# Four output stores moved behind the K loads of batch 2, with a fourth output buffer

## The chip, the cores and the metric

The kernel runs on one core of a Trainium2 chip. A core has TensorE (matrix products), VectorE, ScalarE and GpSimd, SyncE, which here only issues transfers, and 16 DMA engines that move data between HBM (the chip's memory) and SBUF (the core's). ScalarE can issue transfers too, from a queue of its own. The metric is the device time of one execution in microseconds (us); where several runs are given, their median.

In the profile PE is TensorE's product unit, PEld its loading of weights, DVE is VectorE, ACT is ScalarE, POOL is GpSimd, and SPq and ACTq are the DMA-issuing sides of SyncE and ScalarE.

## The reference

Sliding-window causal attention over eight batches of eight heads, 576 positions and 64 columns, and then a layer with a hard-swish over all 4608 positions:

```python
scores = (q @ k.transpose(0, 1, 3, 2)) / sqrt(64)        # (8, 8, 576, 576)
rel = pos[:, None] - pos[None, :]
scores = where((rel >= 0) & (rel < 64), scores, -1e9)
attn = softmax(scores)                                    # over the last axis
x = (attn @ v).transpose(0, 2, 1, 3).reshape(4608, 512)
h = x @ moe_w_in                                          # (4608, 2048)
g = h * clip(h + 3, 0, 6) / 6
out = g @ moe_w_out                                       # (4608, 512), float32
```

## The kernel before

The batches b = 0 to 7 go through attention one after the other, and the layer works on nine blocks T = 0 to 8 of 512 positions. While TensorE multiplies block T in `s1` (x by the first weight, line 767) and `s2` (by the second, line 815), the attention of batch T + 1 is slotted between the products of `s2`.

Inputs arrive as float32 in staging tiles (`st`, six of them, and `tl` for the last 64 rows of a batch), are cast to bf16, and are used from there. Batches 0 and 1 (b < NR6 = 2) are transposed on TensorE. From batch 2 on another way is taken (`load_nat`): four loads and a tail for Q, four loads and a tail for K (line 455, SyncE's queue), a cast of each on GpSimd into `nat` (line 277), and then one DMA transposition for Q and one for K from `nat` into `QKT` (line 434, SyncE's queue). The first scores of the batch (`scores64`, line 648) need both transpositions. The V of such a batch is loaded in five pieces by ScalarE's queue (`stream_v`, line 381), in gaps between its activations. The normalised output of attention (`opg`) goes through four further DMA transpositions into `xT` (line 720, SyncE), which `s1` of the next block reads.

An output tile of 128 x 512 is made in PSUM (`acc`), copied by ScalarE to an SBUF tile `osb` (line 832), and stored to HBM from SyncE's queue (line 837). `osb` has three buffers; copy number `nst` is planned behind store `nst - 3`. Each block T has four such stores; those of T = 0 are the numbers 0 to 3, called stores 1 to 4 below.

The order of the instructions on each engine is fixed when the program is built. The class `Plan` holds a list of work items, each with an engine, a time at which it is ready, a duration and the keys of the items it depends on; it simulates the engines with fixed costs and emits each item when its turn comes. `moved` is its model of the DMA queue, `pl.mark` states that a key is done, and `deps` names the keys to be waited for. An order once emitted is followed on the chip whatever the real times are: each engine takes its instructions in sequence, and an instruction that waits for a semaphore holds up all behind it. The transfers of both queues share eight completion semaphores in rotation, and a transfer waits, before it is issued, until the previous user of its semaphore has landed.

Near the change SyncE's queue before has this order: four Q loads of batch 2, store 1, Q's tail, two K loads, store 2, two K loads, store 3, K's tail, the transposition of Q, store 4, the transposition of K, and then the loads of batch 3.

Of the kernel before, what the change touches and what calls it, by code (L numbers as in the profile page):

```python
# [10 lines left out]
F32 = mybir.dt.float32  # L11
# [9 lines left out]
NSTAGE = 6  # L21
NQT = 1
NPT = 4
VGAP = 1.8
VGAP2 = 1.8
VRATE = 150
# [78 lines left out]
def kernel(  # L105
# [10 lines left out]
    P = nc.NUM_PARTITIONS  # L116
# [5 lines left out]
    KB = (S + P - 1) // P  # L122
    SP = KB * P
# [7 lines left out]
    QW = P + WINDOW  # L131
    VW = D + 1
    scale = 1.0 / math.sqrt(D)
    NR6 = 2
# [3 lines left out]
    pl = Plan()  # L138

    consts = ctx.enter_context(tc.tile_pool(name="consts", bufs=1))  # L140
# [2 lines left out]
    small = ctx.enter_context(tc.tile_pool(name="small", bufs=3))  # L143
    opool = ctx.enter_context(tc.tile_pool(name="opool", bufs=4))
    t1pool = ctx.enter_context(tc.tile_pool(name="t1", bufs=3))
    osbp = ctx.enter_context(tc.tile_pool(name="osb", bufs=3))
    psums = [ctx.enter_context(tc.tile_pool(name=f"ps{i}", bufs=1, space=PSUM)) for i in range(3)]
    early = ExitStack()
    psums.append(early.enter_context(tc.tile_pool(name="ps3", bufs=1, space=PSUM)))
# [24 lines left out]
    neg32 = consts.tile([P, QW], F32, name="neg32")  # L174
    neg = consts.tile([P, TB], BF16, name="neg")
    half = consts.tile([P, 1], F32, name="half")
    mask32 = consts.tile([P, QW], F32, name="mask32")
    m64 = consts.tile([P, D], F32, name="m64")
    mask = consts.tile([P, QW], BF16, name="mask")
    win16 = consts.tile([P, NG, FF], BF16, name="win16")  # L180
# [11 lines left out]

    P_ring = [consts.tile([P, 2, KB, 2 * P], BF16, name=f"pT{i}") for i in range(NPT)]
    V_ring = [consts.tile([P, NG, KB, 2, VW], BF16, name=f"V{i}") for i in range(2)]
# [66 lines left out]
    def stage_slot(casts):  # L261

        stage_hist.append(casts)
        return tuple(stage_hist[-1 - NSTAGE]) if len(stage_hist) > NSTAGE else ()

    def moved(now, kb, rate):

        dma["t"] = max(dma["t"], now) + kb / rate
        land = dma["t"] + 1.9 + dma["lag"]
        return max(now + 0.06, dma["t"] - 5.0), land  # L270

    def cast_op(eng, out_ap, in_ap):
        if eng == "DVE":
            return lambda s: nc.vector.tensor_copy(out=out_ap, in_=in_ap) and None  # L274
        if eng == "ACT":
            return lambda s: nc.scalar.copy(out=out_ap, in_=in_ap) and None  # L276
        return lambda s: nc.gpsimd.tensor_copy(out=out_ap, in_=in_ap) and None  # L277
# [36 lines left out]
    def tail_slot(casts):  # L314
        tail_hist.append(casts)
        return tuple(tail_hist[-4]) if len(tail_hist) > 3 else ()
# [48 lines left out]
    def stream_v(b):  # L365

        V, W = V_ring[b % 2], W_ring[b % 2]
        tiles = {}
        deps = stage_slot([("cast", b, 2, i) for i in range(KB - 1)]) + (("pv", b - 2, NG - 1), ("issued", b, 1 if b == NR6 else 0))
        tdeps = tail_slot([("cast", b, 2, KB - 1)])  # L370

        def issue(kb):
            ss = min(P, S - kb * P)
            def fn(s):
                if kb == 0:
                    tiles["t"] = stage.tile([P, 4, H * D], F32, name="st", tag="st")
                    tiles["l"] = tails.tile([P, H * D], F32, name="tl", tag="tl")
                if kb == KB - 1:
                    pl.mark(("vgo", b), s)
                st = tiles["l"][:ss, :] if kb == KB - 1 else tiles["t"][:, kb, :]  # L380
                nc.scalar.dma_start(
                    out=st.rearrange("p (h d) -> p h d", h=H),
                    in_=v[b, :, kb * P : kb * P + ss, :].rearrange("h s d -> s h d"),
                )
                dma["v"] = max(dma["v"], s) + 262 * ss / P / VRATE
                land = dma["v"] + 2.7
                sv = st.rearrange("p (g h d) -> p g h d", g=NG, h=2)
                todo = [(("POOL",), W[D:P, :, kb, :, 0:D], sv[0:D], H * D)]
                if ss == P:
                    todo.append((("POOL",), V[:, :, kb, :, 0:D], sv, H * D))  # L390
                    todo.append((("POOL",), W[0:D, :, kb + 1, :, 0:D], sv[D:P], H * D))
                casts(("cast", b, 2, kb), land, todo)
                if kb < KB - 1:
                    pl.op("ACT", s + (VGAP2 if b == NR6 else VGAP), 0.45, issue(kb + 1))
            return fn
        pl.op("ACT", 0.0, 0.45, issue(0), deps=deps + tdeps)
# [26 lines left out]
    def load_nat(b):  # L423
        for i, src in enumerate((q, k)):
            T = {"left": KB}
            n = natural[i]
            deps = stage_slot([("cast", b, i, j) for j in range(KB - 1)])
            if b > NR6:
                deps += (("vgo", b - 1),)
            if b > NR6:  # L430
                deps += (("tr", b - 1, i),)
            def tr(t, i=i, n=n):
                def fn(s):
                    nc.sync.dma_start_transpose(
                        out=QK_tiles[b % NQT][:, i * NG : (i + 1) * NG, :].rearrange("d g (k t) -> d (g k) t", t=P),
                        in_=n[:].rearrange("p g k d -> p (g k d)"),
                    )
                    fr, land = moved(s, 655, 230)
                    pl.free["SP"] = fr
                    pl.mark(("issued", b, i), s)  # L440
                    return land
                d = (("S", b - NQT, NG - 1),) if b >= NQT else ()
                if b > 2:
                    d += (("s1", b - 1),)
                pl.op("SP", t, 0.1, fn, ("tr", b, i), deps=d)
            for kb in range(KB):
                ss = min(P, S - kb * P)
                def go(s, i=i, src=src, kb=kb, ss=ss, T=T, n=n, tr=tr):
                    if kb == 0:
                        T["t"] = stage.tile([P, 4, H * D], F32, name="st", tag="st")  # L450
                    if kb == KB - 1:
                        st = tails.tile([P, H * D], F32, name="tl", tag="tl")[:ss, :]
                    else:
                        st = T["t"][:, kb, :]
                    nc.sync.dma_start(
                        out=st.rearrange("p (h d) -> p h d", h=H),
                        in_=src[b, :, kb * P : kb * P + ss, :].rearrange("h s d -> s h d"),
                    )
                    fr, land = moved(s, 262 * ss / P, 205)
                    def done(t):  # L460
                        T["left"] -= 1
                        if not T["left"]:
                            tr(t)
                    pl.op("POOL", land, 0.61,
                          cast_op("POOL", n[:ss, :, kb, :], st.rearrange("p (g d) -> p g d", g=NG)),
                          ("cast", b, i, kb), done)
                    return fr
                yield b, deps + tail_slot([("cast", b, i, kb)]) if kb == KB - 1 else deps, go
        stream_v(b)
# [59 lines left out]
    def ready(f, b, g):  # L529
# [4 lines left out]
        elif f[0] == "S":  # L534
            ks = [("tr", b, g)] if b < NR6 else [("tr", b, i) for i in range(2)]
            if b == 0:
                ks.append("neg")
            if n >= NPT:
                ks.append(("pv", (n - NPT) // NG, (n - NPT) % NG))
        elif f == "PV":  # L540
# [32 lines left out]
    def scores(b, g, which=(0, 1)):  # L573
# [3 lines left out]
        n = b * NG + g  # L577
        pT = P_ring[n % NPT]
        add = b == 0
# [53 lines left out]
    def blocks(b, g):  # L633
        n = b * NG + g
        return P_ring[n % NPT][:].rearrange("p h k w -> p (h k w)")[:, 0 : 2 * S].rearrange("p (h c) -> p h c", h=2)

# [42 lines left out]
    def pv128(b, g, o):  # L679
        V = V_ring[b % 2]  # L680
        pT = P_ring[(b * NG + g) % NPT]
        for h in range(2):
# [142 lines left out]
    def finish(T, ts, acc, c0, c1):  # L825
        u0 = T * TB + ts * P
        nst = T * 4 + ts + (c0 > 0)
        cell = {}
        def cp(s):
            osb = osbp.tile([P, DM], F32, name="osb", tag="osb")  # L830
            cell["o"] = osb
            nc.scalar.copy(out=osb[:, c0:c1], in_=acc[:, c0:c1])  # L832
            if c0:
                nc.scalar.dma_start(out=out[u0 : u0 + P, c0:c1], in_=osb[:, c0:c1])
        def store(t):
            def fn(s):
                nc.sync.dma_start(out=out[u0 : u0 + P, c0:c1], in_=cell["o"][:, c0:c1])
                fr, land = moved(s, 262, 375)
                pl.free["SP"] = fr
                return land  # L840
            pl.op("SP", t, 0.1, fn, ("st", nst))
        pl.op("ACT", pl.t + 0.1, 0.62, cp, ("acc", nst), None if c0 else store,
              deps=(("st", nst - 3),) if nst >= 3 else ())


    next_load(0.0)
# [34 lines left out]
    for T in range(NTB):  # L881
# [3 lines left out]
        b = T + 1  # L885
# [36 lines left out]
```

The softmax here doesn't subtract the row's maximum and nothing guards it: scores larger than these inputs give would overflow.

## Time and profile before

| | us |
|---|---|
| median of 5 runs | 310.81 (310.34 to 312.92) |
| the profiled execution | 311.0 |
| its span in the profile | 309.3 |
| TensorE busy | 296.4 |
| VectorE, ScalarE, GpSimd busy | 161.0, 157.0, 116.1 |

The span is the time from the first to the last instruction in the profile; 1.7 us of the profiled execution lie around it. TensorE's granted clock is 1.00 throughout. A line of the timeline gives the start, the time taken, the engine, the line of the kernel, the operation, what is written and read, the number of instructions merged, and in brackets the idle time before it with what ended it. The stretch that the change concerns, in the same profile, cut in pieces with the busy time of each engine, the clock, the share of the DMA engines and their rate:

```profile
core 0: us, PE busy (x) PEld busy (x) DVE busy (x) ACT busy (x) POOL busy (x), PEclk, DMA share, GB/s
59.20:74.00 14.80, 14.75 (x68) 6.50 (x67) 8.95 (x8) 9.20 (x9) 6.75 (x12) 1.00 1.27 248
74.00:75.20 1.20, 0.07 (x6) 0.07 (x7) 0.88 (x1) 0.29 (x1) 1.07 (x3) 1.00 1.32 201
75.20:92.00 16.80, 16.27 (x209) 8.36 (x214) 7.37 (x13) 6.43 (x11) 9.97 (x15) 1.00 1.15 201
```

TensorE is busy all the time until 74.0, does almost nothing for 1.2 us, and is nearly full again.

The transfers of SyncE around it, with the time from issue to landing where the prediction uses it:

| transfer | issued at | takes to issue | landed at |
|---|---|---|---|
| first Q load of batch 2 | 46.95 | 0.57 | 51.95 |
| store 1 | 52.12 | 1.71 | 56.5 |
| store 2 | 55.89 | 0.88 | 60.1 |
| store 3 | 58.52 | 1.36 | 63.1 |
| K's tail | 59.92 | 0.61 | 64.6 |
| transposition of Q | 60.63 | 4.19 | 68.4 |
| store 4 | 64.95 | 0.50 | 69.95 |
| transposition of K | 65.57 | 4.37 | 75.07 |
| first Q load of batch 3 | 70.46 | 0.40 | 76.96 |

### The profile page before, as it was taken

How to read it: one execution, taken by the hardware profiler on the slowest of the kernel's cores; microseconds unless marked ns; L12 is line 12 of the kernel's file. 1: busy time of each engine (PE TensorE's matmuls, PEld its weight loads, DVE VectorE, ACT ScalarE, POOL GpSimd, SP SyncE). 2: the span in 40 equal slices, each digit the busy share in tenths (PEclk: the TensorE clock that was granted, in tenths of full speed). 3: DMA queues.
4: the chain of work that ended last, by engine and by line, in shares of the span. 5: the costliest groups of instructions: out<-in, count | busy, mean ns of one | idle time of the engine just before them, and what ended most of it. 6: DMA issues, size and time to landing. Idle time of an engine off the chain costs nothing.

```text
span 309.3 us, 6664 instructions
## 1 busy us (share of the span) xinstructions
PE 296.4 (96%) x2746; PEld 153.7 (50%) x2787; DVE 161.0 (52%) x208; ACT 157.0 (51%) x199; POOL 116.1 (38%) x185
## 2 busy tenths in 40 slices
PE   8979999998999999999999999999999999999996
PEld 4544445643544454875444544444665544444443
DVE  5486675566614772468336642675176516404610
ACT  5936677465515651566155724662367236315611
POOL 3167558437824741357127622662261000000000
PEclk9999999999999999999999999999999999999999
DMA  8999999999999998999899999999990520010011
GB/s 231 279 336 389 389 311 210 256 223 238 197 220 241 253 215 161 205 233 214 178 171 257 213 183 205 250 216 159 209 208 29 120 76 0 34 70 35 0 68 70
DMA packets 153487, 58.38 MB, mean 189 GB/s; under 512 B 142064, under 2 KB 143344, under 8 KB 153456
## 3 DMA queue, kind: packets, MB, share of 16 engines
q1 hardware_dynamic: 125184, 50.80, 76.9%
q10 hardware_dynamic: 28272, 7.15, 12.0%
q8 instruction: 22, 0.36, 0.5%
q14 instruction: 9, 0.07, 0.1%
HBM read 36.70 MB, written 9.44 MB: 149 GB/s over the span
## 4 chain that ended last, share of the span: by engine, by line
PE 71%; DMA 18%; POOL 4%; SPq 3%; issue 2%; DVE 0%; ACT 0%; ACTq 0%; POOLq 0%
PE acc L815 35%; PE ps L767 29%; DMA QKT<-nat 6%; DMA st<-in_moe_w_out_dram 5%; PE ps L672 3%; DMA st<-in_v_dram 3%; PE ps L648 3%; DMA st<-in_k_dram 3%; SPq L329 1%; POOL V L277 1%; SPq L412 1%; POOL wout L277 1%; DMA out_dram<-osb 1%; PE ps L737 0%; PE ps L685 0%
## 5 line engine op out<-in xcount | busy, mean ns | idle before, releaser
L779 DVE SCALAR_TENSOR_TENSOR gT<-t,ps 128x1024 bf16<-128x1024 bf16 x72 | 87.6, 1221 | 102.0 <-ACT t L776 102.0
L815 PE MATMUL acc<-wout,gT 128*128 128x512 bf16 (+2 forms) x559 | 129.3, 373 | 3.1 <-issue 2.2
L767 PE MATMUL ps<-xT,win 128*128 128x512 bf16 (+4 forms) x696 | 126.1, 340 | 1.1 <-DVE gT L779 0.6
L776 ACT ACTIVATE t<-ps,half 128x1024 bf16<-128x1024 f32 x72 | 79.8, 1113 | 50.0 <-PE ps L767 47.8
L767 PEld LDWEIGHTS <-win 128*128 128x128 bf16 x704 | 65.2, 98 | 60.6 <-issue 1.5
L815 PEld LDWEIGHTS <-gT 128*128 128x128 bf16 x592 | 53.6, 98 | 57.9
L832 ACT COPY osb<-acc 128x512 f32<-128x512 f32 (+2 forms) x37 | 21.3, 575 | 75.9 <-PE acc L815 66.5
L277 POOL CAST runs<-st 64x512 bf16<-64x512 f32 (+1 forms) x49 | 30.8, 628 | 66.1 <-DMA st<-in_v_dram 55.9
L277 POOL CAST nat<-st 128x512 bf16<-128x512 f32 x48 | 32.1, 676 | 23.0 <-DMA st<-in_k_dram 15.4
L654 ACT ACTIVATE pT<-ps 128x640 bf16<-128x640 f32 (+1 forms) x48 | 28.7, 650 | 10.7 <-PE ps L648 10.7
L713 DVE TENSOR_TENSOR opg<-ps,rec 128x640 bf16<-128x640 f32 x32 | 26.4, 825 | 1.1
L658 DVE TENSOR_TENSOR pT<-pT,mask 128x1152 bf16<-128x1152 bf16 x24 | 20.0, 832 | 7.2 <-ACT pT L654 7.2
L277 POOL CAST V<-st 128x512 bf16<-128x512 f32 (+1 forms) x30 | 19.5, 651 | 3.8 <-DMA st<-in_v_dram 2.3
L602 ACT ACTIVATE pT<-ps 128x768 bf16<-128x768 f32 x16 | 12.6, 841 | 1.3 <-PE ps L593 1.2
L648 PEld LDWEIGHTS <-QKT 64*128 64x128 bf16 x432 | 7.6, 95 | 11.4 <-issue 9.7
L672 PEld LDWEIGHTS <-pT 128*64 128x64 bf16 x480 | 9.5, 111 | 5.7 <-issue 3.0
L672 PE MATMUL ps<-runs,pT 128*64 128x65 bf16 x288 | 12.2, 197 | 0.0
L648 PE MATMUL ps<-QKT 64*128 64x64 bf16 x432 | 10.5, 191 | 1.4 <-DMA QKT<-nat 1.1
L710 DVE RECIPROCAL rec<-ps 128x10 f32<-128x10 f32 x32 | 6.9, 216 | 9.3 <-PE ps L672 7.8
L276 ACT COPY QKT<-ps 128x1152 bf16<-128x1152 bf16 x8 | 9.0, 1135 | 5.0 <-PE ps L562 5.0
L672 PE MATMUL ps<-V,pT 128*64 128x65 bf16 x192 | 11.3, 198 | 0.0
L274 DVE CAST runs<-st 128x576 bf16<-128x576 f32 x14 | 7.2, 520 | 6.0 <-DMA st<-in_q_dram 4.2
(60 smaller groups left out, 119.0 us busy)
## 6 DMA issues: line engine op xcount, KB each, us to landing
out_dram<-osb SPq DMA_DIRECT2D x35, 256.0 KB, 3.5
st<-in_q_dram SPq DMA_DIRECT2D x24, 256.0 KB, 6.0
st<-in_k_dram SPq DMA_DIRECT2D x24, 256.0 KB, 5.1
st<-in_v_dram ACTq DMA_DIRECT2D x24, 256.0 KB, 5.3
st<-in_moe_w_out_dram SPq DMA_DIRECT2D x4, 1024.0 KB, 13.1
st<-in_moe_w_in_dram SPq DMA_DIRECT2D x3, 1024.0 KB, 10.8
st<-in_q_dram SPq DMA_DIRECT2D x8, 288.0 KB, 6.6
st<-in_k_dram SPq DMA_DIRECT2D x8, 288.0 KB, 6.3
```

Of the source, the lines that this page charges most:

```text
L277: return lambda s: nc.gpsimd.tensor_copy(out=out_ap, in_=in_ap) and None
L602: nc.scalar.activation(out=pT[:, :, kbs[0] : kbs[0] + 2, 0:QW], in_=st[:, :, 0 : 2 * QW].rearrange("p h (k w) -> p h k w", k=2), func=EXP, ...
L648: nc.tensor.matmul(st[:, h, c : c + D], lhsT=kwin(b, g, i, h), rhs=QT[h * D : (h + 1) * D, i * D : (i + 1) * D], start=True, stop=True,)
L654: nc.scalar.activation(out=pT[:, :, i0 * D : i1 * D], in_=st[:, :, 0 : (i1 - i0) * D], func=EXP, scale=scale,)
L658: pl.op("DVE", t, 0.8, lambda s: nc.vector.tensor_tensor(out=pT.rearrange("p h (i w) -> p (h i) w", w=D), in0=pT.rearrange("p h (i w) -> p ...
L672: nc.tensor.matmul(o[odd * D : (odd + 1) * D, h, m * VW : (m + 1) * VW], lhsT=pT[:, h, i * D : (i + 1) * D], rhs=(V if i % 2 else W)[:, g, ...
L713: nc.vector.tensor_tensor(out=opg[:].rearrange("p k h d -> p h k d"), in0=ov[:, :, :, 0:D], in1=rec[:].unsqueeze(3).to_broadcast([P, 2, KB ...
L767: nc.tensor.matmul(hT[:, j, dst : dst + w], lhsT=win16[:, g, (2 * c + j) * P : (2 * c + j + 1) * P], rhs=xT[:, g, src : src + w], start=(g ...
L776: nc.scalar.activation(out=t1[:], in_=hT[:], func=RELU, bias=half[:], scale=1.0 / 6.0)
L779: nc.vector.scalar_tensor_tensor(out=gT[:, 2 * c : 2 * c + 2, :], in0=cell["t"][:], scalar=1.0, in1=hT[:], op0=MIN, op1=MULT,)
L815: nc.tensor.matmul(accs[ts][:, c0:c1], lhsT=gT[:, fc, ts * P : (ts + 1) * P], rhs=wout16[:, fc, c0:c1], start=(fc == 0), stop=(fc == NFC - 1),
L832: nc.scalar.copy(out=osb[:, c0:c1], in_=acc[:, c0:c1])
```

## The change

```diff
+NOSB = 4
...
-    osbp = ctx.enter_context(tc.tile_pool(name="osb", bufs=3))
+    osbp = ctx.enter_context(tc.tile_pool(name="osb", bufs=NOSB))
...
-    mask32 = consts.tile([P, QW], F32, name="mask32")
+    mask32 = neg32
...
                     fr, land = moved(s, 262 * ss / P, 205)
+                    if i and kb == KB - 1:
+                        pl.mark(("loads", b), s)
...
-            pl.op("SP", t, 0.1, fn, ("st", nst))
+            pl.op("SP", t, 0.1, fn, ("st", nst), deps=(("loads", NR6),) if T == 0 else ())
         pl.op("ACT", pl.t + 0.1, 0.62, cp, ("acc", nst), None if c0 else store,
-              deps=(("st", nst - 3),) if nst >= 3 else ())
+              deps=(("st", nst - NOSB),) if nst >= NOSB else ())
```

When the tail of K of a batch is emitted, a key `("loads", b)` is marked. The four stores of block 0 now depend on that key for batch 2, so the plan emits them after K's tail. `osb` gets a fourth buffer, and the copies are planned behind the store four back. The float32 tile from which the second mask is made is no longer a tile of its own: it uses `neg32` again, after that has been cast.

The order in the built program differs from before in this. SyncE: four Q loads, Q's tail, four K loads, K's tail, stores 1, 2 and 3, the transposition of Q, store 4, the transposition of K; from the loads of batch 3 on the order is the same. ScalarE: the five V loads of batch 2 each stand one activation earlier. TensorE, VectorE and GpSimd have the same order of instructions. With the order, the assignment of the eight semaphores changes. Waits of the two transpositions, before and after:

```
before  DmaTransposeAnt QKT<-nat (Q) [waits DMAHW6,PE,Pool]   DmaTransposeAnt QKT<-nat (K) [waits DMAHW1,PE,Pool]
after   DmaTransposeAnt QKT<-nat (Q) [waits DMAHW7,PE,Pool]   DmaTransposeAnt QKT<-nat (K) [waits DMAHW2,PE,Pool]
```

Before, the last user of DMAHW1 ahead of the K transposition is the third K load. After, the last user of DMAHW2 ahead of it is the first V load of batch 2.

## The prediction

> **What bounds the kernel now.** I read the page first: engine shares, then the chain of waits, the list of waits for TensorE, and the timeline from 59 to 94 us, queue by queue.
>
> ```profile
> PE 296.4 (96%) x2746; PEld 153.7 (50%) x2787; DVE 161.0 (52%) x208; ACT 157.0 (51%) x199; POOL 116.1 (38%) x185
> ...
> PE 71%; DMA 18%; POOL 4%; SPq 3%; issue 2%; DVE 0%; ACT 0%; ACTq 0%; POOLq 0%
> ```
> TensorE is busy for 96% of the span, and no other engine passes 52%. Time can only be won where TensorE stands still. It stands still longest, after its start, in one place that this change can reach:
> ```profile
> 72.98 1.03 PE L815 MATMUL acc<-wout,gT 128*128 128x512 bf16 x4
> 75.13 0.44 PE L648 MATMUL ps<-QKT 64*128 64x64 bf16 x18 [1.12 <-DMA QKT<-nat]
> ...
> PE ps L648 <- DMA QKT<-nat: 1.1, 1, 1.1
> ...
> PE ps L767 <- DVE gT L779: 0.6, 1, 0.6
> ```
> The first scores of batch 2 wait 1.12 us for the transposed Q and K. The only later idle time above 0.16 us is 0.61 us at 166.46. So the whole prize is 1.1 us, at best 1.7. Which step of the transfer chain is late is in the DMA queue of SyncE:
> ```profile
> 58.52 1.36 SPq L837 DMA_DIRECT2D out_dram<-osb  x1
> 59.92 0.61 SPq L455 DMA_DIRECT2D tl<-in_k_dram  x1
> 60.63 4.19 SPq L434 DMA_TRANSPOSE QKT<-nat  x1
> 64.95 0.50 SPq L837 DMA_DIRECT2D out_dram<-osb  x1
> 65.57 4.37 SPq L434 DMA_TRANSPOSE QKT<-nat  x1
> 70.46 6.54 SPq L455 DMA_DIRECT2D st<-in_q_dram  x4
> ```
> (Columns: start, time to issue, line, what.) The queue is never empty here. The K transposition is issued at 65.57 and lands 9.5 us later, at 75.07; its operand was ready only just before, since the last K cast ran on GpSimd from 64.65 to 65.26:
> ```profile
> 64.65 0.61 POOL L277 CAST nat<-tl 64x512 bf16<-64x512 f32 x1 [1.91 <-DMA tl<-in_k_dram]
> 62.98 0.43 ACTq L381 DMA_DIRECT2D st<-in_v_dram  x1
> 64.55 0.38 ACTq L381 DMA_DIRECT2D st<-in_v_dram  x1
> 66.28 0.68 ACTq L381 DMA_DIRECT2D st<-in_v_dram  x1
> ```
> The last three lines are V loads on ScalarE's queue; they land at 68.1, 69.9 and 73.4. (The chain puts a V load ahead of the K transposition, but that load landed 2.5 us after the issue, so it released nothing.)
>
> [...] The trace agrees from 70.5 to 72.4 us, when the two queues had 64.5% and 63.9% of the engines. It shows more: between 64.5 and 66.0 only SyncE's queue moved data, although two V loads had been issued at 62.98 and 64.55. [...] The program has eight for both queues and reuses them in turn, each transfer waiting for the previous user. The trace shows that such a wait is real: the last V load of batch 2 was issued at 69.88, just when the second V load, the earlier user of its semaphore, landed (69.85).
>
> **The change, part by part.**
>
> Stores. Stores 1 to 3 leave their places among the K loads and are issued after K's tail. Between 46.95 and 60.53 SyncE issues the same 13 transfers, 12.8 us of issue time in all. The Q transposition comes after all of them in both orders, so the order alone wins nothing. The three stores take 1.71, 0.88 and 1.36 us because they queue behind loads; alone a store takes 0.50. In a better order up to 3.95 - 1.5 = 2.4 us could go, but the third store must wait until K's first load has landed and the Q transposition until its third has (about 58 and 59 if they go out 2 us earlier). So the Q transposition starts at 59.2 to 60.6; I take 59.7 (0.9 us won), issues for 4.2 us to 63.9, and store 4 follows to 64.5. K's tail is cast well before that, so the late cast at 65.26 is gone.
>
> V loads. In the changed program ScalarE's order differs in one thing: each V load of batch 2 stands one activation earlier. The first then goes out at 61.09 + 0.16 = 61.25 instead of 62.98, inside the issue of the Q transposition (59.7 to 63.9).
>
> A new wait. The rotation of semaphores changes with the order. Before, the K transposition reuses the semaphore of a K load, long landed. After, it reuses that of the first V load, with a count that includes it. So the K transposition cannot be issued before the first V load has landed. Behind it on SyncE stand the ten loads of batch 3, its output store and the transpositions into xT.
>
> When does that V load land? Before shows four V loads issued inside a transposition's issue as the first of their queue: they land 3.26, 3.44, 3.96 and 4.04 us after the end of that issue (issues ending 64.82, 69.94, 126.29, 158.86; landings 68.08, 73.38, 130.25, 162.90). So 63.9 + 3.4 = 67.3. Bounds: 66.2 (start 59.2, issue 3.8, landing 3.2) and 69.4 (60.6, 4.8, 4.0). Below that, if the load runs in the lull from 62.5 to 64.5 us, where both queues together moved only 77 GB/s, it lands 3.6 us after issue like the one at 88.68: 64.9, and the wait costs nothing.
>
> K transposition. It starts at 67.3 instead of 65.57. Its six executions land 9.5, 8.2, 7.7, 9.1, 7.7 and 8.3 us after issue; the 9.5 is the one before, which shared with V loads from 70.5 on. Now most V loads are ahead of it: I take the mean, 8.4, so 75.7 against 75.07. TensorE has its last ready work at 74.01 in both, so it waits 1.8 us instead of 1.1: +0.7 us.
>
> Later. After the K transposition SyncE is 1.8 us late with the loads of batch 3. These ten took 13.5 us before, and 12.2, 13.4, 11.8 and 14.1 in the later batches. With fewer V loads beside them I take 12.2: they end 0.5 us late. This matters because the last xT transposition of batch 2 lands at 93.44, and TensorE, which begins that block at 92.01, needs it after 14 of 16 products, 1.4 us on, at about 93.45. There is no slack: the loss is the larger of 0.7 (TensorE late) and 0.5 (SyncE late), not the sum, so 0.7. From batch 3 on the slack is there: K lands at 104.1, wanted at 107.0.
>
> At nothing. The fourth buffer: without it the fourth copy (59.41) would wait for store 1, now issued near 58 and landing some 4.4 us later, and ScalarE would stop for 3 us; with it that wait is gone. mask32 sharing neg32: GpSimd's fill at 16.02 must wait for VectorE's casts of neg, done by 3.51. V casts come earlier: before, the last ended at 78.6, and the first product with V began at 79.3.
>
> Sum: +0.7 us on 311.0, this execution's own time (span 309.3 and 1.7 around it). The median shown is 310.8, so I predict 311.5.
>
> **Rivals.**
>
> A. The forecast, a small loss from the new wait, between 310.9 and 312.3.
>
> B. The V load lands in time or the Q transposition starts early; K lands by 74.0, and the 1.1 us are won: 309.7. For it: the lull, and the data of three stores out of the way of K. Against it: all four V loads issued within a transposition landed over 3 us after its end. If the 0.61 us at 166 went too, 309.1.
>
> C. The new wait bites fully, a clear loss: the V load lands at 69.0 (Q transposition from 60.6, issue 4.4, landing 4.0), and the K transposition, with a V load issued 1 us ahead of it, takes 8.4 or more as at 153 (10.1 for the Q one). K then lands at 77.4, TensorE loses 2.3 us: 313.1. It decides from a K landing of 76.6 on. For it: the V load, at 61.25, is bound to fall inside the Q transposition's issue, and two of the four such landings were near 4.0. Against it: SyncE should start early.
>
> D. Nothing moves: the new wait ends at 65.5, with the same landing as before: 310.8.
>
> **How the numbers follow.** A 0.51, B 0.15, C 0.27, D 0.07. The range of 8 in 10 reaches from 309.6, so that B is in it, to 313.0, near the middle of C, and leaves out some 0.16. A change under 0.5% (1.55 us) can't be told from none here. Slower by more, above 312.4: nearly all of C and a seventh of A, 0.34. Faster by more needs both stalls gone: 0.05. The same: 0.61.
>
> **What would show it.** The step on the wait is right if the second QKT transposition on SyncE starts just as the first V load of ScalarE's queue lands, later than 65.57; wrong if it follows store 4 at once. The step on stores is right if the first QKT transposition starts between 59.2 and 60.6. The sum is right if the wait at the first scores of batch 2 grows from 1.12 to some 1.8 us and no new one over 0.5 us appears near 93. A K landing before 74 makes all of it wrong.

## The result and the profile after

The changed kernel took 312.71 us (median of 44 executions, 310.27 to 315.03), the kernel before 312.16 (79 executions, 309.78 to 316.17; the five of the median shown above are among them). The ratio is 1.0024, with a 95% interval of 1.0010 to 1.0039: a loss of some 0.75 us, against a forecast of 0.7. In 22 of the 44 executions TensorE's mean granted clock was 0.995 or lower, and these took 313.69 us in the mean against 312.13 for the others; for the 79 of the kernel before the clock is not on record, so how much of the 0.75 us goes with it is not known. The profiled execution took 312.25 us with a span of 310.5.

The page's busy times and, at the end, the chain that ended last:

```profile
PE 296.2 (95%) x2746; PEld 153.5 (49%) x2787; DVE 161.0 (52%) x208; ACT 157.3 (51%) x199; POOL 116.9 (38%) x185
...
PE 65%; DMA 20%; SPq 8%; POOL 2%; issue 2%; DVE 1%; ACT 1%; ACTq 0%; POOLq 0%
```

TensorE does no more work than before: it is busy 296.2 us against 296.4. The span grew by waiting alone. TensorE's timeline at the first scores of batch 2 and near 94 us, and below it lines of the waits of TensorE (total, times, longest):

```profile
73.32 1.03 PE L818 MATMUL acc<-wout,gT 128*128 128x512 bf16 x4
76.09 0.44 PE L651 MATMUL ps<-QKT 64*128 64x64 bf16 x18 [1.74 <-DMA QKT<-nat]
...
94.45 2.75 PE L770 MATMUL ps<-xT,win 128*128 128x512 bf16 x12 [0.18 <-DMA xT<-opg]
```

```profile
PE ps L651 <- DMA QKT<-nat: 1.7, 1, 1.7
...
PE ps L770 <- DMA xT<-opg: 0.6, 2, 0.4
...
PE ps L770 <- DVE gT L782: 0.2, 1, 0.2
```

The wait for K grew from 1.12 to 1.74 us. The last `xT` transposition lands 0.18 us too late (TensorE now waits for it at 94.45). Of the 1.2 us between the two spans these are 0.62 and 0.18. A further 0.35 lies ahead of everything the change touches (TensorE's wait for V, which ended at 51.96 before, ends at 52.30 after), the stall at 166 us shrank from 0.61 to 0.23, and one of 0.41 appeared at 190. The last three can't be told from chance: TensorE's wait for V near 52 us, before anything that the edits touch, ended anywhere from 51.7 to 54.0 us in the fourteen profiled executions. Nor can the 0.18: in E3 below, with SyncE's order of before, the waits for `xT` near 93 us come to 0.45. So only the first is read as an effect, and even that is the difference of two single executions (see E3).

SyncE's DMA queue (start, time to issue):

```profile
57.74 1.07 SPq L456 DMA_DIRECT2D tl<-in_k_dram  x1
58.90 1.53 SPq L840 DMA_DIRECT2D out_dram<-osb  x3
60.54 4.87 SPq L435 DMA_TRANSPOSE QKT<-nat  x1
65.54 0.54 SPq L840 DMA_DIRECT2D out_dram<-osb  x1
68.66 4.04 SPq L435 DMA_TRANSPOSE QKT<-nat  x1
73.22 3.58 SPq L456 DMA_DIRECT2D st<-in_q_dram  x4
```

The queue was never empty before; now it stands still from 66.08, the end of store 4, to 68.66. The chain of waits, in order of time, says why:

```profile
61.59 6.98 DMA st<-in_v_dram
68.58 0.02 issue
68.60 0.02 POOLq L278
68.62 0.05 issue
68.66 7.38 DMA QKT<-nat
76.05 0.05 issue
76.09 0.44 PE ps L651 x18
```

The first V load of batch 2 lands at 68.58, and K's transposition goes out 0.08 us later. Nothing of what stands behind it on SyncE goes out before it; the loads of batch 3 start at 73.22. In the kernel before, the third K load, the previous user of the semaphore of K's transposition, had landed at 61.2, 4.4 us before K's transposition was issued (65.57). K's operand is no reason, for its last casts on GpSimd were long done:

```profile
61.48 0.61 POOL L278 CAST nat<-st 128x512 bf16<-128x512 f32 x1 [0.59 <-DMA st<-in_k_dram]
62.03 0.61 POOL L278 CAST nat<-tl 64x512 bf16<-64x512 f32 x1
```

The V loads themselves, with ScalarE's activations between them:

```profile
61.44 1.11 ACT L779 ACTIVATE t<-ps,half 128x1024 bf16<-128x1024 f32 x1 [1.14 <-PE ps L770]
61.59 2.02 ACTq L382 DMA_DIRECT2D st<-in_v_dram  x1
63.72 1.11 ACT L779 ACTIVATE t<-ps,half 128x1024 bf16<-128x1024 f32 x1 [1.17 <-PE ps L770]
63.74 1.26 ACTq L382 DMA_DIRECT2D st<-in_v_dram  x1
65.11 1.11 ACT L779 ACTIVATE t<-ps,half 128x1024 bf16<-128x1024 f32 x1 [0.28 <-PE ps L770]
65.13 1.99 ACTq L382 DMA_DIRECT2D st<-in_v_dram  x1
```

The first four V loads took 0.4 to 0.7 us each to issue before; these three take 1.3 to 2.0. The next activation starts only when the load is out (61.59 + 2.02 = 63.61, then 63.72). The bracket names TensorE's `ps`, but ScalarE's own queue is what came last. In this execution the delay of `gT` that follows stayed covered.

### The profile page after: what moved, and what is told of

It reads as the page before. It is cut to its first block, busy times and chain, and to the rows that moved or that the text cites. A ratio compares the mean times of both kernels' runs of the same rounds, so it can differ in the third digit from the quotient of the medians.

```text
span 310.5 us, 6661 instructions
## 1 busy us (share of the span) xinstructions
PE 296.2 (95%) x2746; PEld 153.5 (49%) x2787; DVE 161.0 (52%) x208; ACT 157.3 (51%) x199; POOL 116.9 (38%) x185
## 4 chain that ended last, share of the span: by engine, by line
PE 65%; DMA 20%; SPq 8%; POOL 2%; issue 2%; DVE 1%; ACT 1%; ACTq 0%; POOLq 0%
PE acc L818 31%; PE ps L770 27%; DMA QKT<-nat 6%; DMA st<-in_moe_w_out_dram 5%; DMA st<-in_v_dram 4%; PE ps L675 3%; SPq L355 3%; PE ps L651 3%; DMA xT<-opg 2%; DMA st<-in_q_dram 2%; SPq L330 2%; DMA st<-in_k_dram 2%; SPq L413 1%; SPq L723 1%; SPq L456 1%
## 5 line engine op out<-in xcount | busy, mean ns | idle before, releaser
L278 POOL CAST runs<-st 64x512 bf16<-64x512 f32 (+1 forms) x49 | 30.2, 617 | 69.4 <-DMA st<-in_v_dram 60.2
L278 POOL CAST nat<-st 128x512 bf16<-128x512 f32 x48 | 33.1, 696 | 20.9 <-DMA st<-in_k_dram 12.7
```

## The experiments

Two theories. The first is the prediction's: the loss is the wait of K's transposition for the semaphore of the first V load. The rival: V loads that come one activation early cost the time in themselves, by their data ahead of K's and by holding ScalarE, whatever K's transposition waits for. A third: the loss comes from the stores, the buffer or the mask.

The median of the kernel before was 312.7 us on two of the chips used (E1 to E4, E9 to E11) and 311.4 to 311.5 on two others (E5 to E8, E12), so ratios are compared within a group first. E1 and so on are the runs in the order made. Where a diff begins with `deps` or `pl.mark`, it is against the changed kernel.

**E1: store 4 behind K's transposition.** The semaphores rotate by one, and K's transposition then reuses that of K's tail, which in the changed kernel landed at 61.9.

```diff
-deps=(("loads", NR6),) if T == 0 else ()
+deps=(("loads", NR6) if nst < 3 else ("issued", NR6, 1),) if T == 0 else ()
```

> The changed kernel with store 4 issued after the K transposition of batch 2 instead of before it. The K transposition then reuses the semaphore of K's tail, and no longer that of the first V load; V loads and stores 1 to 3 stay where the change put them. Theory (the loss is the wait for the first V load): the K transposition follows the Q one at once, near 65.5 us, lands at 73 to 74.3, the wait at the first scores of batch 2 falls from 1.74 to under 0.3 us, and the time is 0.996 to 0.999 of before. Rival 1 (the loss is traffic: V loads and store data now beside the transpositions): K lands at 75.5 or later and the ratio is 1.001 or more. Rival 2 (the loss lies elsewhere: fourth buffer, shared mask tile, start): the ratio stays at 1.001 to 1.003.

Ratio 1.0000 (0.9974 to 1.0025). K's transposition follows at once, at 66.54, but lands at 76.04, where it landed in the changed kernel too. TensorE loses its time to something else:

```profile
64.93 4.03 ACTq L382 DMA_DIRECT2D st<-in_v_dram  x1
69.07 1.11 ACT L779 ACTIVATE t<-ps,half 128x1024 bf16<-128x1024 f32 x1 [3.04 <-PE ps L770]
```

```profile
71.49 3.61 PE L770 MATMUL ps<-xT,win 128*128 128x512 bf16 x16 [1.50 <-DVE gT L782]
```

The third V load takes 4.03 us to issue, the activation behind it waits 3.04 us, VectorE's `gT` is late, and TensorE stands for 1.50 us. So with the semaphore wait gone, K lands no sooner. The ratio lies between the two forecasts (0.996 to 0.999, and 1.001 or more); K's landing is that of the rival. The wait for K, 0.14 us, is what the first theory expected, but only because TensorE itself came late. The run was repeated as E12.

**E2: V loads back behind the second activation**, as before the change; stores as changed.

```diff
-pl.mark(("issued", b, i), s)
+pl.mark(("issued", b, i), s + (1.7 if b == NR6 else 0.0))
```

> The changed kernel with the V loads of batch 2 back at their old place, one activation later. The order of SyncE is that of the change, but the K transposition reuses the semaphore of K's tail. Theory (wait for the V load): the K transposition is issued right after store 4, near 66 us, lands at 73.7 to 75.5, the wait at the first scores is 0 to 1.2 us, ratio 0.996 to 1.000. Rival 1 (traffic of the stores ahead of the transpositions): K lands at 75.5 or later, ratio 1.001 or more. Rival 2 (elsewhere): 1.001 to 1.003.

Ratio 0.9994 (0.9968 to 1.0019). The wait for K is 1.01 us, that of the kernel before. The first four V loads take 0.6 us or less to issue again. K landed at 76.3, outside the expected 73.7 to 75.5, but this whole execution runs late: TensorE's wait for V near 52 us ended at 53.33, against 51.96 before. Counted from the issue of Q's transposition, K landed after 14.7 us, against 14.4 before. Stores 1 to 3 behind K's tail win nothing by themselves, and lose nothing.

**E3: only the fourth buffer and the shared mask**, stores where they were.

```diff
-pl.op("SP", t, 0.1, fn, ("st", nst), deps=(("loads", NR6),) if T == 0 else ())
+pl.op("SP", t, 0.1, fn, ("st", nst))
```

> Only the fourth output buffer and the shared mask tile of the change; the stores stay among the K loads. Theory: these cost nothing, ratio 0.999 to 1.001, K transposition issued at 65.6, wait at the first scores 1.0 to 1.3 us. Rival 2 (the loss lies in the buffer, the mask tile or the start of the kernel): ratio 1.002 to 1.003 with the old wait of 1.1 us at the scores. Rival 1 says the same as the theory here.

Ratio 0.9977 (0.9944 to 1.0010): no cost there. The wait for K was 0.27 us in this execution (expected: 1.0 to 1.3), with the order of before, so that wait, taken from one execution, is good to some 0.8 us only. The same execution has a wait of 2.16 us for `gT` at 105.21, with no V load moved.

**E4: all four stores behind K's transposition**, V loads early.

```diff
-deps=(("loads", NR6),) if T == 0 else ()
+deps=(("issued", NR6, 1),) if T == 0 else ()
```

> All four stores of block 0 held back until the K transposition of batch 2 is issued, so both transpositions go ahead of them. Theory: the Q transposition starts near 59, the K one near 63.5, K lands at 71 to 73, no wait at the first scores, ratio 0.996 to 0.998; a loss of some tenths could come back where the last transposition into xT of batch 2 lands. Rival 1 (traffic of V loads): K lands later than 73.5. Rival 2: ratio not under 1.000.

Ratio 1.0039 (1.0011 to 1.0068), slower. Q's transposition starts at 59.74, K's follows, and K lands at 73.08: with a megabyte of stores out of its way that is 13.3 us after the issue of Q's, against 15.5 in the changed kernel. But now V is late. Its tail is issued at 72.97, when the third V load has landed (72.90), and ScalarE's activations stand behind it:

```profile
72.97 0.69 ACTq L382 DMA_DIRECT2D tl<-in_v_dram  x1
73.76 3.12 ACT L779 ACTIVATE t<-ps,half 128x1024 bf16<-128x1024 f32 x3 [3.28 <-DMA out_dram<-osb]
```

```profile
76.18 0.32 PE L651 MATMUL ps<-QKT 64*128 64x64 bf16 x10 [1.35 <-DVE gT L782]
77.31 0.40 PE L651 MATMUL ps<-QKT 64*128 64x64 bf16 x8 [0.81 <-DVE gT L782]
```

(The second line names a store, which landed at 73.61; but the tail, out at 73.66, stands ahead of these activations in ScalarE's order, and the idle time began long before, while the tail waited.) K in time is worth nothing if the products beside the scores have no `gT`.

**E5: the kernel before with V loads alone one activation earlier.** No store moved, no fourth buffer, no semaphore of a V load for K. The diff is against the kernel before.

```diff
-("issued", b, 1 if b == NR6 else 0)
+("vok", b) if b == NR6 else ("issued", b, 0)
...
 pl.mark(("issued", b, i), s)
+if b == NR6 and i == 0:
+    pl.mark(("vok", b), s + 4.5)
```

> The kernel before (stores in their old places, three output buffers) with one thing altered: batch 2's V loads stand one activation earlier on ScalarE, so the first comes after one activation behind copy 4, as in the changed kernel; no V load uses the semaphore of K's transposition. If the loss comes from the earlier V loads themselves (they are issued while a transposition is being issued on SyncE, hold ScalarE's queue, and their data goes ahead of K's): V loads take over 1 us to issue where before they took 0.4 us, and either K's transposition lands at 75.5 us or later or TensorE waits for gT between 66 and 78 us; ratio 1.001 to 1.004. If the loss needs the wait for the semaphore of the first V load: K lands about 75.0, TensorE waits for K 0.3 to 1.1 us, ratio 1.000 or less. If the moved stores cost the time: ratio 1.000.

Ratio 1.0040 (1.0014 to 1.0066). That is the changed kernel's own loss on the same chip (E6), without any part of the change but the place of the V loads. Three of the V loads took 1.0 to 2.2 us to issue, as expected:

```profile
61.78 2.16 ACTq L381 DMA_DIRECT2D st<-in_v_dram  x1
...
64.02 0.99 ACTq L381 DMA_DIRECT2D st<-in_v_dram  x1
...
65.08 2.02 ACTq L381 DMA_DIRECT2D st<-in_v_dram  x1
```

But the expectation of a later K or a wait for `gT` was missed in the one profiled execution: K landed at 75.4, TensorE waited 0.93 us. That execution took 310.95 us, 1.7 below the run's median, so it is not the one to show where the median lost.

**E6: the changed kernel again.**

> The changed kernel once more, on the same chip as its neighbours. Ratio 1.001 to 1.004. First theory (semaphore of the first V load): K's transposition is again issued within 0.15 us after the first V load lands, which is 3.0 to 3.5 us after the end of the issue of Q's transposition; TensorE waits 1.5 to 2.0 us at the first scores of batch 2. If the wait of 1.74 us was chance of that one execution: it is 0.3 to 1.2 us here.

Ratio 1.0041 (1.0013 to 1.0069). This execution took 313.56 us and shows both effects at once:

```profile
61.24 5.38 SPq L435 DMA_TRANSPOSE QKT<-nat  x1
66.75 0.49 SPq L840 DMA_DIRECT2D out_dram<-osb  x1
70.87 3.90 SPq L435 DMA_TRANSPOSE QKT<-nat  x1
```

```profile
65.43 3.23 ACTq L382 DMA_DIRECT2D st<-in_v_dram  x1
68.76 1.11 ACT L779 ACTIVATE t<-ps,half 128x1024 bf16<-128x1024 f32 x1 [2.25 <-PE ps L770]
```

```profile
71.18 3.61 PE L770 MATMUL ps<-xT,win 128*128 128x512 bf16 x16 [0.70 <-DVE gT L782]
78.37 0.43 PE L651 MATMUL ps<-QKT 64*128 64x64 bf16 x18 [2.71 <-DMA QKT<-nat]
```

The first V load landed at 70.78, 4.2 us after the end of the issue of Q's transposition, and K's transposition went out at 70.87. So the wait for that semaphore is real in two executions of two, and its length varies: SyncE stood for 2.58 us in the first and 3.63 here.

**E7: the changed kernel with three buffers** (`NOSB = 3`).

> The changed kernel with three output buffers in place of four. My prediction's claim: copy 4 then waits for store 1, issued behind K's tail at about 58.9 us and landed some 2 to 4 us later (61 to 63), so ScalarE stands still for up to 3 us with five output activations behind it; the planner places copy 4 after the first activation. TensorE waits for gT 1 us or more between 60 and 68 us, ratio to the kernel before 1.004 to 1.010. If store 1 lands early enough or gT is ahead: no wait for gT, ratio 1.001 to 1.004 as the change itself.

Ratio 1.0087 (1.0064 to 1.0110): the moved stores without the fourth buffer are worse, as the prediction had it. But the claimed stop of 3 us was not there. The program puts copy 4 behind the first activation, and it waits 0.75 us for store 1, which landed at 63.07:

```profile
61.29 1.11 ACT L779 ACTIVATE t<-ps,half 128x1024 bf16<-128x1024 f32 x1 [2.66 <-PE ps L770]
63.16 0.59 ACT L835 COPY osb<-acc 128x512 f32<-128x512 f32 x1 [0.75 <-DMA out_dram<-osb]
63.32 0.43 ACTq L382 DMA_DIRECT2D st<-in_v_dram  x1
```

TensorE did not wait for `gT` here. It waited 2.05 us for K, which landed at 76.15. With K's transposition now ahead of store 4, this kernel has no wait for a V load either. Right behind that wait TensorE's granted clock was 0.50 for 3.4 us (from 77.3), which by an estimate from these two figures can have cost up to 1.7 us. What makes up the 0.87% was not found; this execution, at 312.95, lies 1.7 us below the run's median.

**E8: V loads two activations later than before** (`s + 5.1` in E2's edit).

> The changed kernel with batch 2's V loads two activations later than in the kernel before (first V load after the fourth activation, at about 66 us instead of 61.6). If early V loads are what costs K's transposition its time: K's transposition is issued at 65 to 67 us and lands at 73 to 75 us, TensorE waits under 0.6 us at batch 2's first scores, ratio 0.996 to 0.999, unless GpSimd's casts of V, now 2 to 3 us later, hold up the first products with V at 79 us (then a wait for V there, ratio 1.000 to 1.005). If the loss is elsewhere (stores, buffer, mask): ratio 1.001 to 1.004, with K landing at 76 us.

Ratio 1.0119 (1.0069 to 1.0169). The first half came as expected: K landed at 74.88 and TensorE waited neither for it nor for `gT`, the only run of which that is true. The second half cost more than expected:

```profile
81.29 0.19 PE L675 MATMUL ps<-runs,pT 128*64 128x65 bf16 x1 [0.91 <-POOL runs L278]
81.97 0.19 PE L675 MATMUL ps<-V,pT 128*64 128x65 bf16 x1 [0.49 <-POOL V L278]
84.67 0.27 PE L675 MATMUL ps<-runs,pT 128*64 128x65 bf16 x3 [2.51 <-POOL runs L278]
```

Three waits for casts of V, 3.9 us in sum. And during the third of them the granted clock (the column after the five engines) falls to half for 6.8 us:

```profile
83.20:89.90 6.70, 4.90 (x57) 2.55 (x58) 1.69 (x4) 1.19 (x2) 5.13 (x9) 0.50 0.82 164
```

All six executions of this run had a mean clock of 0.995 or lower, so its ratio is that of the waits and of the clock together. V has a due time as well, and the place it had before is between the two.

**E9 and E10: store 4 behind K's transposition with V loads in the old place.** E9 is the edits of E1 and E2 together; in E10 stores 1 to 3 are in their old places too.

```diff
-deps=(("loads", NR6),) if T == 0 else ()
+deps=(("issued", NR6, 1),) if T == 0 and nst == 3 else ()
```

> The changed kernel with batch 2's V loads back behind the second activation, as before the change, and with store 4 behind K's transposition, so that K's transposition follows Q's at once. If the place of the V loads is the whole loss, and store 4's 0.5 to 0.9 us ahead of K's transposition is worth something: K's transposition is issued at the end of Q's issue (64.5 to 66.5 us), lands 0.5 to 1 us earlier than with V back alone, TensorE waits 0 to 0.6 us at batch 2's first scores, ratio 0.996 to 0.999. If transpositions and V data share what moves them, so that the sum of their times is fixed: K lands at 75 to 76 us whatever its issue, ratio 0.999 to 1.001.

> Stores 1 to 3 and the V loads in the places of the kernel before, a fourth output buffer, and only store 4 held until K's transposition is issued. Same two cases: K lands 0.5 to 1 us earlier than before, wait 0 to 0.6 us, ratio 0.996 to 0.999; or K lands at 75 to 76 us all the same, ratio 0.999 to 1.001.

Ratios 1.0009 (0.9982 to 1.0036) and 1.0002 (0.9972 to 1.0032). K landed at 75.04 and 75.23, waits 0.36 and 0.94 us. The second case of each expectation holds. Counted from the issue of Q's transposition, K's is issued 0.5 us sooner than in E2 (E9) and 0.35 sooner than before (E10), and lands 0.7 and 0.3 sooner; the ratios show none of it. In E9 what was won at K was lost at `xT` (0.66 us at 93.0 and 1.59 at 95.6).

**E11: V loads one activation later than before** (`s + 3.4`).

> The changed kernel with the first V load of batch 2 behind the third activation (at about 64.5 us), one later than in the kernel before, two later than in the changed kernel. If earlier V loads cost K and later ones cost the products with V: K lands at 74 to 75 us with a wait of 0 to 0.6 us, GpSimd's casts of V end some 1 to 2 us later than before and TensorE waits 0.5 to 2.5 us for V between 79 and 85 us; ratio 0.999 to 1.005. If V has slack of one activation: no wait for V, ratio 0.996 to 0.999.

Ratio 1.0016 (0.9990 to 1.0043). K landed at 75.68, outside the expected 74 to 75, with a wait of 1.28; the wait for V was 0.46 (expected: 0.5 to 2.5). Not distinguishable from the place of before.

**E12: E1 again.**

> The kernel of the first experiment again: V loads one activation early, K's transposition straight behind Q's and without the wait for a V load. It measured a ratio of 1.0000 [0.9974, 1.0025], against 1.0040 [1.0014, 1.0066] for the kernel before with V alone one activation early, which has no such wait either. If the early V loads are the loss with or without the wait: ratio 1.002 to 1.005, a V load of 2 us or more to issue, and TensorE loses 1.3 to 2.5 us to K or gT between 70 and 78 us. If the wait is needed for the loss once the stores are moved: ratio 0.998 to 1.001, and less than 1.3 us lost there.

Ratio 1.0071 (1.0047 to 1.0094), above the expected 1.005: the loss is there without the semaphore wait. The third V load took 3.27 us to issue, and TensorE lost 1.19 and 0.22 us to `gT`. E1 and E12 are one kernel on two chips, and their intervals don't overlap; so the size of this loss differs between chips or sessions by more than an interval says. Why, no run tells.

All runs together. "V" is the number of activations between copy 4 and the first V load; the fourth column is the time from the issue of Q's transposition to the landing of K's; the last is TensorE's waits for K and `gT` (and in E11 `pT`) from 60 to 79 us of the profiled execution.

| run | V | ratio | Q issued to K landed | TensorE waits |
|---|---|---|---|---|
| before | 2 | | 14.4 | 1.12 |
| E3 buffer only | 2 | 0.9977 | 14.3 | 0.27 |
| E2 stores 1 to 3 moved | 2 | 0.9994 | 14.7 | 1.01 |
| E10 store 4 moved | 2 | 1.0002 | 14.2 | 0.94 |
| E9 all four moved | 2 | 1.0009 | 14.0 | 0.36 |
| the change, E6 | 1 | 1.0024, 1.0041 | 15.5, 17.1 | 1.74, 3.41 |
| E5 no store moved | 1 | 1.0040 | 14.6 | 0.93 |
| E1, E12 no wait for V | 1 | 1.0000, 1.0071 | 15.1, 14.3 | 1.93, 1.41 |
| E4 stores last | 1 | 1.0039 | 13.3 | 2.16 |
| E11 | 3 | 1.0016 | 15.0 | 2.36 |
| E8 | 4 | 1.0119 | 12.8 | 0 |

E7, with its V loads at 63.3 and later, is left out of the table. With V at 2 four arrangements of the stores lie within 0.23% of no change; with V at 1 five measurements of six lost 0.24 to 0.71%, and E1 nothing.

## Why the prediction was right, and where it was not

Direction and size came out, and the wait on which the forecast rested is there in both traces of the changed kernel. Whether that wait makes the loss is another question, taken up after the steps. The absolute 311.5 is 1.2 us under the 312.71, because the kernel before itself came to 312.16 rather than 310.81; it is the difference that agrees.

- *Stores.* "The order alone wins nothing" is right (E2). The taken start of Q's transposition, 59.7, is wrong: 60.54, just inside the stated range. The three stores did get cheaper, 1.35 us to issue instead of 3.95, but the ten Q and K loads took 11.0 us instead of 8.9 in their place. This is the term that was mis-sized: all thirteen transfers took 12.35 us to issue instead of 12.83. From the first Q load of batch 2 to Q's transposition it was 13.20 us against 13.68, so 0.5 won rather than 0.9. That stores take long to issue because they queue behind loads is not shown: behind all ten loads these three took 0.45 us each in the mean.
- *V loads.* The place is right, 61.59 for 61.25. What the prediction left out is that these loads can take long to issue in their new place, 1.3 to 2.0 us here and up to 4.0 (E1), and hold up ScalarE's activations. In the profiled execution this cost nothing; in E1, E6 and E12 it cost TensorE 0.70 to 1.79 us by late `gT`.
- *A new wait.* Right: landing of the first V load 3.18 us after the end of Q's issue (taken: 3.4; E6: 4.2), K's transposition right behind it. That 3.4 was near owes something to luck: it was read from four V loads, but the same trace has one issued at 92.12, just after the start of another transposition, which landed 2.2 us after the end of that issue, and one issued at 158.99 which landed right at its end. K's transposition starts at 68.66 rather than 67.3, since Q's started 0.84 later and took 0.67 longer to issue. That is inside the bounds, 66.2 to 69.4.
- *K transposition.* The landing took 7.4 us, not 8.4, so that K came at 76.06 for 75.7: two errors of 1.4 and 1.0 us that nearly cancelled. TensorE's wait, 1.74 for 1.8, is near in part by luck: its last work ended at 74.35, 0.34 later than taken, and the sum's own figures give 75.7 - 75.07 = 0.63, not 0.7. In E6 K landed at 78.33, which is rival C's case (from 76.6 on), and TensorE lost 3.41 us: the two profiled executions fall one to A and one to C.
- *Later.* SyncE's loads of batch 3 ended 0.74 us late (0.5 taken). The wait for the last `xT` transposition was 0.18 us, within what E3 shows with the order of before.
- *At nothing.* Fourth buffer and mask cost nothing (E3), and TensorE had no wait for the V casts in the changed kernel. That the buffer is needed is right (E7), but the stop of ScalarE was 0.75 us, not 3. Not in the sum at all was TensorE's clock. In E4, E7, E8 and E9 it was halved for 3.4 us (E8: 6.8) within 1.2 us of the end of a wait, though not after E6's wait of 2.71 us. By an estimate from the 0.50 such a stretch costs up to half its length. Whether the waits bring it on, and so whether it is part of the loss, no run shows.

What the prediction took for the cause is thus at most one of two ways in which the cause acts. The runs point to the place of the V loads: moved alone, they lost 0.40% where the whole change lost 0.41% (E5, E6, same chip), and moved back, they left the change without loss (E2). This is likely, not proven. The runs without loss and those with it come mostly from different chips: on the chip of E2 the early V loads of E1 lost nothing either, on the chips of E5, E6 and E12 no kernel with the V loads in their old place was run besides the kernel before, and E1 and E12 show that one kernel's ratio can differ by 0.7% between two chips. Nor does E5's one trace show its loss. The semaphore wait shows in both traces of the changed kernel, but taking it away did not bring the time back reliably (E1 1.0000, E12 1.0071) and did not bring K in earlier in E1. What share of the loss it has is left open, and so is how the rest divides between V's data ahead of K's and the hold-up of ScalarE.

That V loads move at all when stores are held back is a side effect of the planner: its model has K's transposition issued earlier, and batch 2's V loads follow that mark.

What makes the issues of the early V loads long (1.3 to 2.0 us in the changed kernel, 4.03 in E1) is open. The transposition that was being issued on SyncE did not hold the first one back to its end: in the changed kernel Q's is being issued from 60.54 to 65.41, and the first V load is through at 63.61. Nor is a transposition under issue enough to make a load's issue long. Later in the same execution a V load falls inside one and takes 0.38 us, as the first two V loads of batch 2 did before the change (0.43 and 0.38):

```profile
128.07 3.90 SPq L435 DMA_TRANSPOSE QKT<-nat  x1
...
128.44 0.38 ACTq L382 DMA_DIRECT2D st<-in_v_dram  x1
```

And the third V load's issue goes on to 67.12, though SyncE issues nothing from 66.08 to 68.66.

No version beat the kernel before: E3 and E2 have the lowest ratios, and their intervals hold 1.

## What to carry to other kernels

When a scheduler orders the work, compare every engine's order before and after, and price what moved without being meant to: here the stores that were meant cost nothing, and the time was most likely lost by the loads on another queue, one activation earlier. Bringing a transfer out earlier need not bring it in earlier (E1: K's transposition out 2.5 us sooner after Q's than in the changed kernel, in 0.4 sooner; the share of the DMA engines from 60 to 76 us was 1.28 before and 1.22 in the changed kernel); where less data stood in front of K it took 13.3 us (E4) and 12.8 (E8), but then the displaced data missed its own due time. A DMA on ScalarE's queue held up the activation behind it until it was out (changed kernel: out at 63.61, the next activation at 63.72; E1: 68.96 and 69.07), so read its time to issue in the trace wherever such a DMA is moved to: the third V load of batch 2 took 0.68 us in the kernel before and 4.03 in E1.

## What the runs showed of the hardware that was not expected

- A plain load of 256 KB on ScalarE's queue took 0.37 to 0.46 us to issue in 23 of 24 cases in the kernel before and in 20 of 24 in the changed one, inside the issue of a transposition on SyncE's queue too (0.38 us at 128.44 in the changed kernel). Batch 2's V loads in their early place took up to 2.0 us in the changed kernel, 3.2 in E6 and 4.0 in E1; ScalarE's next activation started only after them (0.11 us after the first in the changed kernel and after the third in E1).
- With the V loads early, the first of batch 2 landed 3.2 us (changed kernel) to 4.5 us (E4) after the end of the issue of Q's transposition, inside which it had been issued. It was not so everywhere: in the kernel before, one issued at 158.99, inside another transposition's issue, landed at 164.29, right at its end (164.28).
- TensorE's granted clock was 0.50 for 3.4 us in E4 (from 77.0), E7 (77.3) and E9 (96.0) and for 6.8 us in E8 (83.1), each time within 1.2 us of the end of a wait of TensorE. Of the executions of the kernel before that were run beside E1 to E12, 21 of 196 had a mean clock of 0.995 or lower; of the changed kernel's, 22 of 44 in the first result and 3 of 14 in E6.
- A transposition of Q or K took 3.1 (E8) to 5.7 us (before, at 153.13) to issue.
- One kernel's ratio differed by 0.7% between two chips (E1, E12), with intervals of ±0.25% each.
